# Reordering VectorE in the spectral part, and three small moves at the end of the block loop

## The chip, the cores and the metric

The kernel runs on one core of a Trainium2 chip. The metric is the device time of one launch in microseconds, the median of several runs. Times inside the kernel come from one profiled execution and count from its start. The engines are named as in the profile: PE is TensorE (with PEld for its weight loads), DVE is VectorE, ACT is ScalarE, POOL is GpSimd, SP is SyncE, which only issues transfers here.

## The reference

```python
xn = _layernorm(x)                      # x: 2048 x 512
out = x + fnet(xn) + peer(xn)

def fnet(x):     # real part of a DFT over the hidden and the sequence axis
    a = einsum("bsd,ed->bse", x, dft_hid_re); b = einsum("bsd,ed->bse", x, dft_hid_im)
    return einsum("ts,bse->bte", dft_seq_re, a) - einsum("ts,bse->bte", dft_seq_im, b)

def peer(x):     # 32 heads, two sets of 64 keys, 2 of 64 x 64 = 4096 experts for each head
    q = einsum("nd,dhc->nhc", x, w_q)
    s1 = einsum("nhd,ed->nhe", q[..., :128], k1); s2 = einsum("nhd,ed->nhe", q[..., 128:], k2)
    # best 2 of s1 and of s2, best 2 of their 4 sums: experts top_e, weights g = softmax(top_s)
    act = gelu(einsum("nd,nhkd->nhk", x, u[top_e]))
    return einsum("nhk,nhk,nhkd->nd", g, act, v[top_e])
```

## The kernel before

The kernel has three parts, one after the other, that overlap a little at their borders.

The spectral part takes the first 72 us. The DFT matrices are symmetric, so rows can be added and subtracted in pairs ("folded") ahead of a smaller matmul. The 16 tiles of x are held as four groups g of four tiles, taken in the order G = (1, 0, 2, 3). For each group, `ln` takes statistics (L295, L296), the square root on ScalarE (L300), and a chain of five small VectorE steps up to `rstd` and `negm` (L301 to L305); then ScalarE normalises the four tiles (L317), with two of the first group's on VectorE (L264). `fold(k, g)` adds or subtracts the tiles (L348, into the tile `ft`, which has one buffer), folds twice more (`fold_d`, L332 to L339) and writes the two halves of `Q` (`q`, L351 and L352). `main(k, g)` multiplies Q by the DFT matrix (L371), for k = 0 the cosine part and for k = 1 the sine part. One more row, x5, is folded by `fold_row`. After the last `fold(0, g)` the products are evicted, the scales of the query weights are taken from maxima, and the transposed x (`xpose`) is made for the next part.

The score part computes s = x M for the eight groups of heads (L799), where M is the product of the query weights and the keys, and picks the best two of each set. It ends at 443 us.

The block loop treats 14 blocks of 128 tokens densely, over all 4096 experts; the last two blocks are gathered expert by expert beside it, by GpSimd's transfers. For a block b there are:

- z, in eight steps `cg` of 48 matmuls each (`u_part`, L959), with the GELU on ScalarE (L962);
- four gate products (`g_mm`): VectorE builds two one-hot matrices L (L983) and one weighted R (L991, L994), from the constants io_lam and io_c, and 32 matmuls (L996) put the gates of 32 tokens into PSUM, in one of two buffers;
- four gated products (`w_part`): VectorE multiplies gate and GELU (L1007), ScalarE writes the high half in 16 bits (L1012), VectorE the low half (L1015), which frees the gate's buffer. The two halves are put after the next step, through the list `split`;
- v, in eight steps of 12 matmuls (`v_part`, L1024), which needs all four gated products; and `finish` (L1039), which reads v and adds it to the output row.

The loop runs v of block b and then z of block b + 2. In the steps of v lie the first two gated products of block b + 1 (dictionary `vw`), in those of z its third and fourth (`uw`); `vg` and `ug` place the gate products in the same way. The last two blocks have no z after them.

Beside this the loop checks that the input has the symmetry that the folding assumes and that scaled values stay in range. Those are two streams of small units (`units` with 41, `fit_units` with 60). A call of `paced` in each step of z, and of v of the blocks 1 to 11 and half of block 13, issues so many units that the stream ends with its 94th call: z of the last block with z ends at the 92nd. A unit's load goes to SyncE's queue at once; its work on VectorE (such as L755 and L761) follows two steps later and ScalarE's two after that. `verdict` turns all into a flag, and slower code behind it runs only if the flag is set.

Small tiles in PSUM come from the pools `pc` and `pb`, with two buffers each. In the loop `pc` holds v, two of the eight z steps and one row that the gathered blocks use throughout; `pb` holds the other six z steps and the transposed gates.

The order of the instructions on each engine comes from a planner: it goes through the program as it is traced, and at each point of its own reckoning gives an engine the earliest traced instruction that is ready. An order can be forced with a dependency that makes no semaphore, only an order (`NoSync`). `follow`, `hold` and the new `pace` make such.

## Time and profile before

| what | value |
|---|---|
| median of 3 runs | 1100.72 us (1099.63 to 1101.38) |
| the profiled execution | 1098.52 us, its span 1096.7 us |
| busy share PE, DVE, ACT, POOL | 97%, 87%, 65%, 55% |
| mean granted clock of TensorE | 0.99 |

The span is the time from the first to the last instruction on the core; the time of the execution also has what lies around it. Busy times leave out instructions that only wait, branch or issue transfers. The timeline's rows give start, time, engine, line, operation, what is written and read, and in brackets how long the engine was idle ahead of it and what ended that. A row may merge several like instructions (x22), and its time is then from the first start to the last end. The granted clock is the share of its full speed at which TensorE was let run.

### The profile page before, as it was taken

What the parts mean: (1) busy time and instruction counts of PE and PEld (TensorE: products, weight loads), DVE (VectorE), ACT (ScalarE), POOL (GpSimd) and SP (SyncE); (2) the same over time, 40 slices, a digit from 0 to 9 for tenths busy, and PEclk for the clock granted to TensorE, in tenths of its full rate; (3) what the DMA queues carried; (4) which work ended last, traced back from release to release, by engine and by line L of the source; (5) the groups of instructions that cost most, each with busy time, mean ns of one, the idle gap of its engine ahead of it and who ended that gap; (6) DMA issues with size and microseconds to landing.
All of it is one profiled execution on the core that took longest, in us unless ns stands there. A gap on an engine that the chain in (4) does not pass through costs nothing.

```text
span 1096.7 us, 28484 instructions
## 1 busy us (share of the span) xinstructions
PE 1064.2 (97%) x11070; PEld 694.1 (63%) x11070; DVE 956.3 (87%) x2748; ACT 716.4 (65%) x1326; POOL 600.4 (55%) x553
## 2 busy tenths in 40 slices
PE   5799999999999999999999999999999999999997
PEld 4254555444544544896786867769678585876943
DVE  6879797979999999976998999889999899799971
ACT  3576557688797858542767667677667666767740
POOL 0023446588887955220657476675566657566522
PEclk9799999999999999999999999999999999999998
DMA  8248152445435241272677677766786767676611
GB/s 330 85 152 309 36 196 97 168 141 212 174 125 205 99 160 65 79 257 72 213 227 220 180 217 238 243 213 188 239 252 197 220 204 240 214 226 199 205 35 46
DMA packets 84936, 196.78 MB, mean 179 GB/s; under 512 B 10770, under 2 KB 27559, under 8 KB 84792
## 3 DMA queue, kind: packets, MB, share of 16 engines
q1 hardware_dynamic: 63898, 123.55, 33.5%
q0 software_dynamic: 20736, 71.31, 21.8%
q8 instruction: 88, 1.44, 0.5%
q14 instruction: 56, 0.46, 0.1%
q10 hardware_dynamic: 158, 0.01, 0.0%
HBM read 177.74 MB, written 17.10 MB: 178 GB/s over the span
## 4 chain that ended last, share of the span: by engine, by line
PE 77%; DVE 14%; issue 3%; ACT 2%; DMA 1%; POOL 1%; SPq 0%; DVEq 0%; POOLq 0%; ACTq 0%
PE s L799 25%; PE v L1024 24%; PE z L959 20%; PE g L996 3%; DVE L L983 2%; PE m L147 2%; PE p L371 2%; DVE vals L807 1%; DVE idx L811 1%; DVE act L1015 1%; DMA cx<-in_cb_dram 1%; DVE ga L1066 1%; DVE cx L755 1%; DVE g L1007 1%; DVE R L991 1%
## 5 line engine op out<-in xcount | busy, mean ns | idle before, releaser
L799 PE MATMUL s<-m,xq 128*128 128x512 f16 x1536 | 338.9, 379 | 0.0
L959 PE MATMUL z<-xb,u 128*128 128x128 f16 x5376 | 306.8, 219 | 0.1
L1024 PE MATMUL v<-v,act 128*128 128x512 f16 x1344 | 300.6, 380 | 3.5 <-DVE act L1015 2.6
L959 PEld LDWEIGHTS <-u 128*128 128x128 f16 x5376 | 301.5, 98 | 3.0 <-issue 0.2
L1084 POOL TENSOR_TENSOR ov<-ov,ga 128x512 f32<-128x512 f32 x128 | 180.8, 1413 | 192.0 <-ACT ga L1079 170.4
L799 PEld LDWEIGHTS <-xq 128*128 128x128 f16 x1536 | 148.3, 98 | 171.3 <-issue 0.2
L1024 PEld LDWEIGHTS <-act 128*128 128x128 f16 x1344 | 128.6, 98 | 152.2 <-DVE act L1015 4.1
L983 DVE TENSOR_TENSOR L<-io_lam,cmp 128x2048 f16<-128x2048 f16 x112 | 149.4, 1343 | 37.2 <-PE g L996 37.2
L1050 POOL DMA_INDIRECT ga<-in_uv_dram,eix x128 | 154.9, 1210 | 48.1 <-POOL ov L1084 36.4
L807 DVE MAX8 vals<-ss 128x8 f32<-128x64 f32 x1024 | 152.5, 216 | 16.4 <-ACT ss L804 16.3
L962 ACT ACTIVATE act<-z,scl 128x512 f32<-128x512 f32 x112 | 76.1, 681 | 102.5 <-PE z L959 102.3
L811 DVE FIND_INDEX8 idx<-vals,ss 128x8 uint16<-128x256 f32 x256 | 107.1, 418 | 0.0
L804 ACT ACTIVATE ss<-s,wsc 128x512 f32<-128x512 f32 x112 | 75.5, 680 | 43.3 <-PE s L799 34.0
L1079 ACT ACTIVATE ga<-ga,za 128x512 f32<-128x512 f32 x128 | 92.0, 721 | 9.3 <-ACT za L1077 0.4
L1012 ACT ACTIVATE act<-g 128x1024 f16<-128x1024 f32 x56 | 73.3, 1311 | 24.5 <-DVE g L1007 24.4
L1066 DVE SCALAR_TENSOR_TENSOR ga<-ga,px 128x512 f32<-128x512 f32 x128 | 85.6, 676 | 0.1
L781 ACT ACTIVATE cx<-cx 128x896 f32<-128x896 f32 x64 | 60.6, 946 | 37.7 <-DVE cx L761 19.0
L1015 DVE TENSOR_TENSOR act<-g,act 128x1024 f16<-128x1024 f32 x56 | 72.8, 1301 | 4.6 <-ACT act L1012 4.4
L1007 DVE SCALAR_TENSOR_TENSOR g<-act,scl,g 128x1024 f32<-128x1024 f32 x56 | 71.4, 1279 | 2.3 <-PE g L996 1.4
L169 POOL TENSOR_TENSOR wq<-wq,wh 128x1024 f16<-128x1024 f32 x26 | 55.5, 2135 | 23.7 <-DMA cx<-in_ca_dram 16.1
L991 DVE TENSOR_TENSOR R<-io_c,cmp 128x1024 f16<-128x1024 f16 x56 | 59.6, 1065 | 0.0
L996 PEld LDWEIGHTS <-L 128*128 128x128 f16 x1792 | 51.7, 96 | 8.0 <-DVE act L1015 1.8
(281 smaller groups left out, 1287.8 us busy)
## 6 DMA issues: line engine op xcount, KB each, us to landing
cx<-in_cb_dram SPq DMA_DIRECT2D x50, 448.0 KB
wq<-in_wq_dram SPq DMA_DIRECT2D x32, 512.0 KB
fit<-in_wq_dram SPq DMA_DIRECT2D x28, 512.0 KB
uv<-in_ut_dram SPq DMA_DIRECT2D x16, 512.0 KB
uv<-in_vn_dram SPq DMA_DIRECT2D x16, 512.0 KB
cx<-in_cb_dram SPq DMA_DIRECT2D x28, 224.0 KB
xq<-in_x_dram SPq DMA_DIRECT2D x8, 512.0 KB
xt_d<-xq SPq DMA_DIRECT2D x16, 256.0 KB
```

Of the source, the lines that this page charges most:

```text
L799: mm = nc.tensor.matmul(ps, xt[i][:, l, kd, :], m[:, r, kd, :], start=(n == 0), stop=(n == 3 * KD - 1))
L807: nc.vector.max(vals[:, i, w, :, h], s[:, g, :])
L811: nc.vector.max_index(idx[:, i, w].rearrange("p k h -> p (k h)"), vals[:, i, w, 0:2].rearrange("p k h -> p (k h)"), s[:, w * HC:g + 1, :]. ...
L959: mm = nc.tensor.matmul(p[:, cc * P:(cc + 1) * P], ug[:, l, c % 2, kd, :], xb[:, r, kd, :], start=(n == 0), stop=(n == 3 * KD - 1))
L983: nc.vector.tensor_tensor(L.rearrange("p t (l two) -> p t l two", two=2), io_lam.rearrange("p (l two) -> p l two", two=2).unsqueeze(1).to_ ...
L996: i = nc.tensor.matmul(p[:, hf, t * NC:(t + 1) * NC], L[:, t, :], R[:, hf * 16 + t, :], start=True, stop=True)
L1015: nc.vector.tensor_tensor(w16[..., 1], w, w16[..., 0], op=ALU.subtract)
L1024: mm = nc.tensor.matmul(pv, w16[:, c, :, l], vg[:, r, c % 2, :], start=(c == 0 and k == 0), stop=(c == NC - 1 and k == 2))
L1050: nc.gpsimd.indirect_dma_start(out=t, out_offset=None, in_=uv, in_offset=bass.IndirectOffsetOnAxis(ap=eix[:, n].rearrange("p k h -> p (k h ...
L1066: nc.vector.scalar_tensor_tensor(t, t, 1.0, T["x"], op0=ALU.mult, op1=ALU.mult, accum_out=T["z", n][:, s:s + 1])
L1079: nc.scalar.activation(t, t, AF.Copy, scale=z)
L1084: T["a"] = nc.gpsimd.tensor_tensor(o, o, t, op=ALU.add)
```

## The change

Seven edits in three groups.

In the spectral part: the constants io_lam, io_c, ident16 and not0 are no longer converted on VectorE at the start but after the first group's negm (`constants`), and the iota for two of them comes after the identity on GpSimd. For the groups 0 and 2 the first step of the fold (`fold_t`) is split off; the next group's whole `ln` is traced after it, and the rest of the fold is put behind that group's negm (`end`). The fold of the extra row for k = 1 is put behind the fold traced last (`FF["end"]`).

In the diff, `i` in `fold_d` and in `fold_row` is the first instruction of each.

In the block loop: the fourth gated product of each block with z after it is placed in z's step 3 instead of 4, so that its halves come after step 4 instead of 5. The last block's v is taken from `pb` instead of `pc`.

The checks: the streams end with the 90th call instead of the 94th.

```diff
-    with tc.tile_pool(name="iop", bufs=1, side="right") as iop:
-        iof = iop.tile([P, P], F32, name="iof")
-        nc.gpsimd.iota(iof, pattern=[[1, P]], base=0, channel_multiplier=0,
-                        allow_small_or_imprecise_dtypes=True)
-        nc.vector.tensor_copy(io_lam, iof)
-        nc.vector.tensor_scalar(io_c, iof[:, :NC], float(P), None, op0=ALU.mult)
...
     make_identity(nc, ident)
-    nc.vector.tensor_copy(ident16, ident)
-    nc.vector.tensor_scalar(not0, ident[:, 0:1], -1.0, 1.0, op0=ALU.mult, op1=ALU.add)
+    iof = da.tile([P, P], F32, name="iof")
+    nc.gpsimd.iota(iof, pattern=[[1, P]], base=0, channel_multiplier=0,
+                   allow_small_or_imprecise_dtypes=True)
+
+    def pace(i, after):
+        tc.add_manual_dep(i.ins, after.ins.name, mybir.DependencyInfo(
+            mybir.DependencyClass.NoSync, mybir.DependencyReason.DATA), reason="pace")
+
+    def constants(after):
+        for i in (nc.vector.tensor_scalar(not0, ident[:, 0:1], -1.0, 1.0, op0=ALU.mult, op1=ALU.add),
+                  nc.vector.tensor_copy(ident16, ident), nc.vector.tensor_copy(io_lam, iof),
+                  nc.vector.tensor_scalar(io_c, iof[:, :NC], float(P), None, op0=ALU.mult)):
+            pace(i, after)
...
-        nc.vector.scalar_tensor_tensor(negm[:, g], mvs[:, g, :, 0], -1.0, rstd[:, g], op0=ALU.mult, op1=ALU.mult)
+        end = nc.vector.scalar_tensor_tensor(negm[:, g], mvs[:, g, :, 0], -1.0, rstd[:, g], op0=ALU.mult, op1=ALU.mult)
...
+        return end
...
-    def fold_d(k, t, f, o):
+    def fold_d(k, t, f, o, after=None):
...
+        if after is not None:
+            pace(i, after)
...
+    def fold_t(k, g):
         op = ALU.subtract if k else ALU.add
         t = FF["t"] = da.tile([P, 2, 512], F32, tag="ft", name=f"ft{k}_{g}", bufs=1)
+        nc.vector.tensor_tensor(t, xn[g][:, 0:2], xn[g][:, 2:4], op=op)
+
+    def fold(k, g, after=None):
+        if after is None:
+            fold_t(k, g)
...
-        nc.vector.tensor_tensor(Q[k][g][:, 1, c], o[:, 0, c], o[:, 1, c], op=ALU.subtract)
+        FF["end"] = nc.vector.tensor_tensor(Q[k][g][:, 1, c], o[:, 0, c], o[:, 1, c], op=ALU.subtract)
...
     def fold_row(k):
...
+        if k:
+            pace(i, FF["end"])
...
     for n, g in enumerate(G):
-        ln(g, n)
+        if n == 0:
+            constants(ln(g, n))
+        elif n == 1:
+            ln(g, n)
         if n == 3:
             fold(1, G[0])
             fold_row(0)
             main_row()
-        fold(0, g)
+        if n in (1, 2):
+            fold_t(0, g)
+            fold(0, g, ln(G[n + 1], n + 1))
+        else:
+            fold(0, g)
         main(0, g)
...
-            for f in st[0][st[2]:-(-len(st[0]) * st[1] // (8 * (NB - 2) - 2))]:
+            for f in st[0][st[2]:-(-len(st[0]) * st[1] // (8 * (NB - 2) - 6))]:
...
-            pv = pc(f"v{b}")
+            pv = (pb if b + 1 == NB else pc)(f"v{b}")
             if b + 2 < NB:
-                vw, vg, uw, ug = {0: 0, 4: 1}, {1: 1, 5: 2}, {0: 2, 4: 3}, {1: (1, 3), 5: (2, 0)}
+                vw, vg, uw, ug = {0: 0, 4: 1}, {1: 1, 5: 2}, {0: 2, 3: 3}, {1: (1, 3), 5: (2, 0)}
```

More of the change, by code (lines that the diff above doesn't have):

```diff
@@ L330, in halves @@
             return v.rearrange("p q (s c) -> p q s c", s=2)
-        nc.vector.tensor_tensor(halves(f)[..., 1:P], halves(t[:, :, 0:256])[..., 0:P - 1],
+        i = nc.vector.tensor_tensor(halves(f)[..., 1:P], halves(t[:, :, 0:256])[..., 0:P - 1],
                           halves(t[:, :, 256:512])[..., 1:P], op=op)
+        if after is not None:
+            pace(i, after)
         c = 256 - P * k
@@ L339, in fold_d @@
         nc.vector.tensor_tensor(o[:, :, P + k:2 * P], f[:, :, k:P], f[:, :, P + k:], op=po)
-    def fold(k, g):
+    def fold_t(k, g):
         op = ALU.subtract if k else ALU.add
         t = FF["t"] = da.tile([P, 2, 512], F32, tag="ft", name=f"ft{k}_{g}", bufs=1)
+        nc.vector.tensor_tensor(t, xn[g][:, 0:2], xn[g][:, 2:4], op=op)
+    def fold(k, g, after=None):
+        if after is None:
+            fold_t(k, g)
         f = da.tile([P, 2, 256], F32, tag="ff", name=f"ff{k}_{g}", bufs=2)
         o = FF[k, g] = da.tile([P, 2, 257], F32, tag="fo", name=f"fo{k}_{g}", bufs=2)
-        nc.vector.tensor_tensor(t, xn[g][:, 0:2], xn[g][:, 2:4], op=op)
-        fold_d(k, t, f, o)
+        fold_d(k, FF["t"], f, o, after)
         c = slice(k, 257 - k)
         nc.vector.tensor_tensor(Q[k][g][:, 0, c], o[:, 0, c], o[:, 1, c], op=ALU.add)
-        nc.vector.tensor_tensor(Q[k][g][:, 1, c], o[:, 0, c], o[:, 1, c], op=ALU.subtract)
+        FF["end"] = nc.vector.tensor_tensor(Q[k][g][:, 1, c], o[:, 0, c], o[:, 1, c], op=ALU.subtract)
     def fold_row(k):
         r = da.tile([1, 1, 768], F32, tag="r5", name=f"r5_{k}")
-        nc.vector.tensor_tensor(r[:, 0, 0:512], x5[:, 0], x5[:, 1], op=ALU.subtract if k else ALU.add)
+        i = nc.vector.tensor_tensor(r[:, 0, 0:512], x5[:, 0], x5[:, 1], op=ALU.subtract if k else ALU.add)
+        if k:
+            pace(i, FF["end"])
         fold_d(k, r[:, :, 0:512], r[:, :, 512:], Q[1][0][0:1, 0:1] if k else s5.unsqueeze(1))
```

## The prediction

> **What bounds the kernel now.** I read the page first, then who waited for whom on the TensorE, then the timeline around each of those waits. The page's first line shows a TensorE that is nearly always busy, so a change can only take away its idle time or its slow clock.

> ```profile
> PE 1064.2 (97%) x11070; PEld 694.1 (63%) x11070; DVE 956.3 (87%) x2748; ACT 716.4 (65%) x1326; POOL 600.4 (55%) x553
> ```

> The waits of the TensorE (in all, times, longest) say where the idle time lies:

> ```profile
> PE p L371 <- DVE q L351: 10.0, 4, 3.5
> PE v L1024 <- DVE act L1015: 2.6, 2, 2.1
> PE g L996 <- DVE act L1015: 1.3, 1, 1.3
> PE v L1024 <- DVE y L1039: 0.8, 1, 0.8
> ```

> So there are two places. In the spectral part the matmuls wait four times for VectorE's folds: VectorE is the bound there. In the block loop all that is left is 4.7 us in four waits, each one behind a VectorE result. The change touches all of these. I sum against the profiled execution's 1098.52 us (span 1096.7), which lies 2.2 under the median of 1100.72; the predicted time is that median plus the sum.

> **Spectral part, the constants.** Timeline, columns: start, time from first start to last end, engine, line:

> ```profile
> 8.10 0.68 DVE L295 BATCH_NORM_STATS2 st<-xq 128x6 f32<-128x512 f32 x1
> 9.48 0.43 DVE L80 CAST io_lam<-iof 128x128 f16<-128x128 f32 x1 [0.70 <-POOL iof L78]
> 9.62 0.31 DVE L81 TENSOR_SCALAR io_c<-iof 128x32 f16<-128x32 f32 x1
> 10.31 0.17 DVE L296 BATCH_NORM_AGGREGATE mvs<-st 128x2 f32<-128x6 f32 x1
> 13.40 1.22 DVE L348 TENSOR_TENSOR ft<-xq 128x1024 f32<-128x1024 f32 x1 [0.67 <-ACT xq L317]
> ```

> The last statistics end at 8.10 + 0.68 = 8.78, but their aggregate starts at 10.31, behind four conversions that wait for GpSimd. All later VectorE work of this part hangs on that aggregate. With the conversions moved behind negm it can start at 8.78: **1.53 us sooner**. They cost nothing again: VectorE has 0.67 us free before ft, and without their waits four conversions need about 0.14 us each by the starts at 9.48 and 9.62, some 0.55. If that cover is gone, they cost 0.55. On GpSimd the iota for two of them now comes behind the identity; both were done ahead of the row at 10.31, and are now wanted only after negm, a chain of 1.29 (below) later.

> **Spectral part, the order.** Four groups g (order 1, 0, 2, 3) are normalised and folded; the fourth's fold (0,3) releases the long run of 24 matmuls.

> ```profile
> 14.66 0.69 DVE L332 TENSOR_TENSOR ff<-ft 128x508 f32<-128x508 f32 x1
> 16.59 0.42 DVE L352 TENSOR_TENSOR q<-fo 128x257 f32<-128x257 f32 x1
> 17.05 1.29 DVE L295 BATCH_NORM_STATS2 fo<-xq 128x6 f32<-128x512 f32 x2
> 19.65 0.30 DVE L296 BATCH_NORM_AGGREGATE mvs<-fo 128x2 f32<-128x6 f32 x2
> 19.99 0.30 ACT L300 ACTIVATE sm<-mvs,eps 128x4 f32<-128x4 f32 x1 [5.12 <-DVE mvs L296]
> 21.12 0.16 DVE L305 SCALAR_TENSOR_TENSOR negm<-mvs,rstd 128x4 f32<-128x4 f32 x1
> 24.15 1.51 ACT L320 ACTIVATE x<-x,negm,rstd 1x512 f32<-1x512 f32 x2
> 24.74 1.21 DVE L348 TENSOR_TENSOR ft<-xq 128x1024 f32<-128x1024 f32 x1
> 25.96 0.65 DVE L357 TENSOR_TENSOR r<-x 1x512 f32<-1x512 f32 x1
> 38.84 0.14 DVE L305 SCALAR_TENSOR_TENSOR negm<-mvs,rstd 128x4 f32<-128x4 f32 x1
> 39.02 2.93 ACT L317 ACTIVATE xq<-xq,negm,rstd 128x512 f32<-128x512 f32 x4 [4.51 <-DVE negm L305]
> 41.98 1.23 DVE L348 TENSOR_TENSOR ft<-xq 128x1024 f32<-128x1024 f32 x1 [1.86 <-ACT xq L317]
> 46.32 12.44 PE L371 MATMUL p<-c,q 128*128 128x512 f32 x24 [3.22 <-DVE q L351]
> ```

> From these rows the pieces undisturbed: four statistics 17.05 to 19.95 = 2.90; square root to negm 19.99 to 21.28 = 1.29; ft 1.21; the rest of a fold 14.66 to 17.01 = 2.35. Before, the small steps of one group's negm are spread between another group's folds: the last negm comes at 38.98, VectorE then runs dry for 1.86 while ScalarE normalises (2.93), and only then comes the fourth ft. After, negm of the next group goes ahead of the fold, so ScalarE's 2.93 lies beside fold work.

> Worked out: second ft ends at 24.74 + 1.21 - 1.53 = 24.4. ScalarE is through with the row x at 24.15 + 1.51 - 1.53 = 24.1, so the square root starts there, negm of group 2 ends at 25.4. Fold rest 2.35: 27.8. Statistics of group 3 (2.90), ft of group 2 (1.21), chain 1.29: negm of group 3 at 33.2. The extra row's fold (0.65 and some 0.9 behind it, an estimate from its smaller shapes) goes into the holes of the chains or adds up to 1.6; I take half: 34.0, against 38.98. ScalarE is done at 36.9. From 34.0 VectorE has the rest of (0,2) 2.35, all of fold (1,1) 3.56, since ft has one buffer and is handed on in order, ft 1.21, and 2.0 to the first q: 43.1, against 46.32. That is -3.2; the last two steps of (1,1), 0.7, may fall behind, and the row's fold vanish in holes (-0.8). I take **-3.5 for both edits together**. Ends: -1.0 (order costs 0.5, since a chain with nothing beside it leaves holes: two chains of 1.29) and -5.0 (all filled). After q the run of 24 matmuls, evictions and maxima hang on the same q, so they move along; the score matmuls behind them are dense, so nothing gives it back. The stores of the transposed rows and the loads behind them in SyncE's queue follow the transposes and move with them.

> **Block loop, the fourth gated product.** The one large wait, on its way from z to v:

> ```profile
> 828.04 5.34 PE L1024 MATMUL v<-v,act 128*128 128x512 f16 x24
> 839.60 10.88 PE L959 MATMUL z<-xb,u 128*128 128x128 f16 x192
> 847.00 2.35 DVE L983 TENSOR_TENSOR L<-io_lam,cmp 128x2048 f16<-128x2048 f16 x2
> 850.32 0.95 PE L996 MATMUL g<-R,L 128*128 128x32 f16 x32
> 854.99 1.76 DVE L755 TENSOR_TENSOR cx<-cx 128x256 f32<-128x256 f32 x2 [2.15 <-DMA cx<-in_cb_dram]
> 857.81 1.29 DVE L1015 TENSOR_TENSOR act<-g,act 128x1024 f16<-128x1024 f32 x1
> 859.16 6.56 PE L1024 MATMUL v<-v,act 128*128 128x512 f16 x22 [2.08 <-DVE act L1015]
> 859.00:863.00 4.00, 3.84 (x11) 1.43 (x12) 3.97 (x10) 3.48 (x9) 1.99 (x3) 0.57 0.75 217
> ```

> L1015, the low half of the fourth product, stands in VectorE's queue behind a check (L755) whose transfer is 2.15 late. A step of z is 48 matmuls, 2.7 us by the row of 192; with the halves one step sooner L1015 goes right behind L983, near 849.4, ahead of the check. The 2.08 go. So does what came with them: the last row (a window: PE, PEld, DVE, ACT, POOL busy, then the granted clock) shows 0.57 after the wait, and 22 matmuls took 6.56 where 24 take 5.34, so 22 should take 4.90: 1.66 more. Together **-3.7** (ends 0 and -3.7). What is late next is the check itself; it holds VectorE 0.9 instead of 2.15.

> [...]

> The other such wait, with what VectorE does before it:

> ```profile
> 619.47 2.35 DVE L983 TENSOR_TENSOR L<-io_lam,cmp 128x2048 f16<-128x2048 f16 x2
> 621.54 0.95 PE L996 MATMUL g<-R,L 128*128 128x32 f16 x32
> 628.86 4.92 PE L1024 MATMUL v<-v,act 128*128 128x512 f16 x22 [0.57 <-DVE act L1015]
> 640.00:660.00 20.00, 20.00 (x263) 14.53 (x262) 20.00 (x32) 14.25 (x31) 16.70 (x13) 1.00 0.77 221
> ```

> Here VectorE is full (20.00 of 20). The second L ends at 621.82 and the 17th gate matmul needs it at 621.54 + 0.48 = 622.02: 0.2 to spare. If L1015 (1.29) goes between the two, the gate product waits 1.1; if not, 0.57 are won. I take **0** (ends +1.1 and -0.6).

> **The last blocks.**

> ```profile
> 1049.67 1.02 DVE L755 TENSOR_TENSOR cx<-cx 128x256 f32<-128x256 f32 x2
> 1051.21 1.27 DVE L1015 TENSOR_TENSOR act<-g,act 128x1024 f16<-128x1024 f32 x1
> 1052.53 0.96 PE L996 MATMUL g<-R,L 128*128 128x32 f16 x32 [1.31 <-DVE act L1015]
> 1068.10 20.88 PE L1024 MATMUL v<-v,act 128*128 128x512 f16 x96 [0.84 <-DVE y L1039]
> 1089.02 0.75 DVE L1039 SCALAR_TENSOR_TENSOR y<-v,scl,y 128x512 f32<-128x512 f32 x1 [2.23 <-PE v L1024]
> ```

> Bank: the last v waits 0.84 until VectorE has read the one before out of its bank. The other pair was freed by z long ago: **-0.8** (ends 0, -0.84); the tail behind L1039 moves along. Checks: of 41 units the last was issued in the last z's eighth step and worked on in v of block 12, at 1049.67, ahead of the L1015 for which the gate matmuls wait 1.31. With 90 for 94 steps it is issued eight steps sooner. The wait shrinks by the check's 1.02: **-0.9** (ends 0, -1.31). The price: by 700, some 35 of its steps, 41 units over 90 instead of 94 steps make two thirds of a unit more, 1 to 2 us of VectorE each by the rows of L755, in a stretch that is full: **+0.3** (ends 0, +1.5); its transfers and the halves of u and v read by ScalarE come at most four calls sooner on their queues.

> **Sum:** -3.5 - 3.7 + 0 - 0.8 - 0.9 + 0.3 = **-8.6**: 1089.9 for the profiled execution, 1092.1 for the median. I predict 1092.

> **The rivals.** (1) VectorE stays the bound at the handover: what it is relieved of at L1015 comes back at the next L or check, so that the fourth product gives nothing. For it: 20.00 of 20; against: 847.00's L ends a microsecond before its matmuls. -8.6 + 3.7 = -4.9: 1095.8. (2) The reordering doesn't do what it says: the queue order comes out so that only half of the constants' gain is left (-1.0), and rival 1 holds: -1.0 + 0 - 0.8 - 0.9 + 0.3 = -2.4, at best barely measurable: 1098.3; with the check's wait staying, 1099.2, no change. (3) Slower: L1015 lands between the two L in all twelve z blocks of the loop, and each pays 1.1 as at 621.54: +13.2 - 8.6 = +4.6, 1105.3. It decides from eight blocks on. Against it: at 847.00 both L are done at 849.35, and with 1.29 more the second still ends at 850.64, before the 17th matmul of a gate product that starts at 850.3. (4) More: everything at its good end, -5.0 - 3.7 - 0.6 - 0.8 - 1.3 = -11.4: 1089.3.

> **Chances.** Forecast 0.50 (own range 1090 to 1094.5), rival 4 0.13, rival 1 0.17, rival 2 0.10, rival 3 0.10. A measurement of this kernel can tell about 0.2%, 2.2 us, from no change: faster below 1098.5. Rivals 4 and 1 and the forecast are faster, and rival 2 is split: faster 0.82, same 0.07, slower 0.11. The range takes in rivals 4 and 1, the good end less the 1.1 by which the fastest run lies under the median, and the better half of rival 2: 1088 to 1098.5.

> **What would show it.** The first mvs aggregate near 8.8 and the four conversions after negm; the fourth ft near 39, without a wait for ScalarE; 24 matmuls starting near 43; L1015 before the next L1012 by a step, no wait of v for it, and a clock of 1.00 through 850 to 870; no wait of v for y; the wait of g at 1051 under 0.5. The prediction is wrong if g waits for L in many blocks, if the fourth ft still waits for ScalarE, or if the run of 24 starts after 45.

## The result, and the profile after

In six runs each, the kernel before took 1100.27 us in the median (1098.56 to 1103.19) and the changed one 1092.67 us (1091.40 to 1094.45). The ratio is 0.9936, with a 95% interval of 0.9913 to 0.9958: 7.0 us less, give or take 2.5. The forecast was 1092.0. The profiled execution of the changed kernel took 1093.28 us (span 1091.4), 5.2 less than that of before. So part of the gain between the medians does not show between the two traces; the profiled execution of before was one of its better ones.

The first line of the page after, and who waited for whom on TensorE (us in all, times, longest):

```profile
PE 1062.2 (97%) x11070; PEld 694.0 (64%) x11070; DVE 979.0 (90%) x2748; ACT 716.2 (66%) x1326; POOL 603.7 (55%) x553
```

```profile
PE p L385 <- DVE q L363: 7.7, 3, 4.9
PE z L980 <- DVE y L1060: 2.0, 3, 1.1
PE g L1017 <- DVE L L1004: 1.6, 3, 0.7
PE g L1017 <- DVE act L1036: 0.9, 1, 0.9
PE m L141 <- POOL wq L163: 0.9, 1, 0.9
```

The lines have new numbers: L1060 is the `y` of `finish` (L1039 before), L1004 the L (L983), L1036 the low half (L1015), L353 the first step of a fold (L348), L776 a check's work (L755). Both waits of v, for the low half and for y, are gone. New are a wait of z for y, which I had not thought of, and a longer one of the gate product for L. Where the time went, by the first matmul of each part:

| from the start to | before | after | difference |
|---|---|---|---|
| first score matmul | 72.45 | 69.43 | -3.03 |
| first z matmul, the start of the block loop | 443.89 | 441.45 | -2.44 |
| end of the last v matmul | 1088.98 | 1084.87 | -4.11 |
| end of the span | 1096.72 | 1091.38 | -5.34 |

The spectral part gains 3.0 and gives 0.6 back in the score part; the block loop gains 1.7; after the last matmul 1.2 more go. The timeline after (start, time, engine, line), first the spectral part with the one wait of the score part:

```profile
8.82 0.18 DVE L301 BATCH_NORM_AGGREGATE mvs<-st 128x2 f32<-128x6 f32 x1
12.03 1.23 DVE L353 TENSOR_TENSOR ft<-xq 128x1024 f32<-128x1024 f32 x1 [0.19 <-ACT xq L322]
24.72 0.67 DVE L369 TENSOR_TENSOR r<-x 1x512 f32<-1x512 f32 x1
26.77 0.16 DVE L310 SCALAR_TENSOR_TENSOR negm<-mvs,rstd 128x4 f32<-128x4 f32 x1
33.91 0.16 DVE L310 SCALAR_TENSOR_TENSOR negm<-mvs,rstd 128x4 f32<-128x4 f32 x1
38.58 1.22 DVE L353 TENSOR_TENSOR ft<-xq 128x1024 f32<-128x1024 f32 x1
43.46 12.11 PE L385 MATMUL p<-c,q 128*128 128x512 f32 x24 [0.85 <-DVE q L363]
86.50 0.20 PE L141 MATMUL m<-sums,wq 128*128 128x64 f16 x1 [0.88 <-POOL wq L163]
```

It went as worked out: the aggregate at 8.82 (before 10.31), the extra row's fold in the hole of a chain, the last negm at 33.91, the fourth ft at 38.58 with no wait for ScalarE, the run of 24 at 43.46. Then the loop, with four of its waits:

```profile
620.08 0.56 PE L1017 MATMUL g<-R,L 128*128 128x32 f16 x16 [0.73 <-DVE L L1004]
621.21 0.56 PE L1017 MATMUL g<-R,L 128*128 128x32 f16 x16 [0.57 <-DVE L L1004]
702.47 1.72 PE L980 MATMUL z<-xb,u 128*128 128x128 f16 x28 [1.15 <-DVE y L1060]
853.65 1.30 DVE L1036 TENSOR_TENSOR act<-g,act 128x1024 f16<-128x1024 f32 x1
854.85 1.90 DVE L776 TENSOR_TENSOR cx<-cx 128x256 f32<-128x256 f32 x2
1049.42 0.97 PE L1017 MATMUL g<-R,L 128*128 128x32 f16 x32 [0.92 <-DVE act L1036]
```

At 853.65 the low half goes ahead of the check that had held it up, and the check's load is no longer late. Two windows over the whole loop, of before and of after, in this order (us, then busy time and count of PE, PEld, DVE, ACT, POOL, the granted clock, the share of DMA, GB/s):

```profile
443.90:1089.00 645.10, 640.02 (x8551) 478.62 (x8548) 568.66 (x876) 409.10 (x851) 351.72 (x276) 1.00 0.64 196
```

```profile
441.50:1084.90 643.40, 638.62 (x8551) 478.75 (x8547) 588.78 (x876) 409.28 (x851) 355.29 (x276) 1.00 0.65 196
```

TensorE is idle for 645.10 - 640.02 = 5.1 before and 643.40 - 638.62 = 4.8 after. So in these two traces the waits were exchanged, not saved. What fell is TensorE's busy time, by 1.4, and the slow clock after the wait at 857 (0.50 from 859.09 to 862.50), 1.7 by the forecast's reckoning, accounts for that. The forecast's three gains in the loop cannot all have come as they were argued, although the total fits.

### The profile page after: what moved, and what is told of

Its sections match the earlier page's. It is cut to its first block, busy times and chain, and to the rows that moved or that the text cites. A ratio compares the mean times of both kernels' runs of the same rounds, so it can differ in the third digit from the quotient of the medians.

```text
span 1091.4 us, 28485 instructions
## 1 busy us (share of the span) xinstructions
PE 1062.2 (97%) x11070; PEld 694.0 (64%) x11070; DVE 979.0 (90%) x2748; ACT 716.2 (66%) x1326; POOL 603.7 (55%) x553
## 5 line engine op out<-in xcount | busy, mean ns | idle before, releaser
L1105 POOL TENSOR_TENSOR ov<-ov,ga 128x512 f32<-128x512 f32 x128 | 177.7, 1388 | 185.3 <-ACT ga L1100 164.5
L1071 POOL DMA_INDIRECT ga<-in_uv_dram,eix x128 | 162.1, 1266 | 48.4 <-POOL ov L1105 35.5
L1004 DVE TENSOR_TENSOR L<-io_lam,cmp 128x2048 f16<-128x2048 f16 x112 | 159.5, 1438 | 17.7 <-PE g L1017 17.7
L983 ACT ACTIVATE act<-z,scl 128x512 f32<-128x512 f32 x112 | 75.6, 680 | 92.0 <-PE z L980 88.5
L1036 DVE TENSOR_TENSOR act<-g,act 128x1024 f16<-128x1024 f32 x56 | 72.9, 1301 | 7.9 <-ACT act L1033 7.4
L1015 DVE TENSOR_TENSOR R<-R,cmp 128x1024 f16<-128x1024 f16 x56 | 59.4, 1062 | 1.4
```

Source lines behind the costliest of these rows:

```text
L1004: nc.vector.tensor_tensor(L.rearrange("p t (l two) -> p t l two", two=2), io_lam.rearrange("p (l two) -> p l two", two=2).unsqueeze(1).to_ ...
L1036: nc.vector.tensor_tensor(w16[..., 1], w, w16[..., 0], op=ALU.subtract)
L1071: nc.gpsimd.indirect_dma_start(out=t, out_offset=None, in_=uv, in_offset=bass.IndirectOffsetOnAxis(ap=eix[:, n].rearrange("p k h -> p (k h ...
L1105: T["a"] = nc.gpsimd.tensor_tensor(o, o, t, op=ALU.add)
```

## Experiments

All ratios are to the kernel before, run on the same chip beside it; 0.001 is 1.1 us.

**The spectral part alone, then its constants alone.** The first kernel is the changed one with the loop's three edits taken back; the second also has the old order:

```diff
-            for f in st[0][st[2]:-(-len(st[0]) * st[1] // (8 * (NB - 2) - 6))]:
+            for f in st[0][st[2]:-(-len(st[0]) * st[1] // (8 * (NB - 2) - 2))]:
...
-            pv = (pb if b + 1 == NB else pc)(f"v{b}")
+            pv = pc(f"v{b}")
...
-                vw, vg, uw, ug = {0: 0, 4: 1}, {1: 1, 5: 2}, {0: 2, 3: 3}, {1: (1, 3), 5: (2, 0)}
+                vw, vg, uw, ug = {0: 0, 4: 1}, {1: 1, 5: 2}, {0: 2, 4: 3}, {1: (1, 3), 5: (2, 0)}
```

```diff
-        if k:
-            pace(i, FF["end"])
...
-        elif n == 1:
+        else:
             ln(g, n)
...
-        if n in (1, 2):
-            fold_t(0, g)
-            fold(0, g, ln(G[n + 1], n + 1))
-        else:
-            fold(0, g)
+        fold(0, g)
```

> The changed kernel with the three edits of the block loop undone: only the constants and the order of the spectral part are left. Theory A (the parts add): the run of 24 matmuls starts near 43.5, where it does with all edits, the first scores 3.0 us earlier than before, 0.6 of it given back at the first weight product, so 2.4 us faster than before, near 1097.9 beside 1100.3; the block loop keeps the waits of before, v for the low half 2.6 us in all, v for y 0.8. Theory B (the spectral part's gain is lost behind it, the whole gain is the loop's): within 1 us of before, although the run of 24 starts earlier.

> Of all edits only the constants behind negm; the order of folds and chains as before. My prediction's step: the first aggregate at 8.8, everything behind it 1.5 us sooner, the run of 24 matmuls near 44.8, the time 1.0 to 1.5 us lower than before. Rival: the chains wait for ScalarE and for normalised tiles anyway, and the run of 24 starts at 45.8 or later: under 0.5 us.

Measured: 0.9963 (0.9935 to 0.9990) for both edits, 0.9982 (0.9957 to 1.0007) for the constants alone. The timeline of the first, then of the second:

```profile
43.55 12.26 PE L385 MATMUL p<-c,q 128*128 128x512 f32 x24 [0.85 <-DVE q L363]
```

```profile
37.68 0.14 DVE L310 SCALAR_TENSOR_TENSOR negm<-mvs,rstd 128x4 f32<-128x4 f32 x1
40.82 1.23 DVE L353 TENSOR_TENSOR ft<-xq 128x1024 f32<-128x1024 f32 x1 [1.86 <-ACT xq L322]
45.16 13.48 PE L383 MATMUL p<-c,q 128*128 128x512 f32 x24 [1.53 <-DVE q L363]
```

The run of 24 comes at 43.55 and at 45.16, against 46.32. So in these traces the constants give 1.2 of what I put at 1.53, and the order another 1.6; in the other kernels with the old spectral part the run starts at 46.5 to 47.2, in those with the new one at 43.5 to 44.1. With the constants alone the fourth ft waits its old 1.86 for ScalarE; only the order takes that away. How long the 24 then run hangs on the clock: they take 12.26 with half clock for 3.4 us of it, 13.48 with 5.9, and 12.44 with 3.8 in before; less half of these times, that is 10.5 to 10.6 in each (an estimate). The 0.6 that I expected to be given back in the score part did not show in the kernel with the spectral part alone. Over all kernels of this study, the start of the block loop lies 0.5 us after that of before in the mean of the six with the old spectral part, before itself among them (-0.3 to +1.3), and 2.9 ahead of it in the mean of the seven with the new one (1.6 to 4.5). That makes 3.4, and the interval of the ratio 1.1 to 7.2; the forecast had 3.5.

**The loop alone.** The kernel before with the three loop edits:

```diff
-            for f in st[0][st[2]:-(-len(st[0]) * st[1] // (8 * (NB - 2) - 2))]:
+            for f in st[0][st[2]:-(-len(st[0]) * st[1] // (8 * (NB - 2) - 6))]:
...
-            pv = pc(f"v{b}")
+            pv = (pb if b + 1 == NB else pc)(f"v{b}")
...
-                vw, vg, uw, ug = {0: 0, 4: 1}, {1: 1, 5: 2}, {0: 2, 4: 3}, {1: (1, 3), 5: (2, 0)}
+                vw, vg, uw, ug = {0: 0, 4: 1}, {1: 1, 5: 2}, {0: 2, 3: 3}, {1: (1, 3), 5: (2, 0)}
```

> The kernel before with the three edits of the block loop and nothing of the spectral part. Theory A: the wait of v for the low half and the slow clock behind it go (3.7 us), the bank and the checks give 1.4, new waits of g for L and of z for y take 3 back: 2 to 3 us faster than before in a profiled run that had the clock's fall, 4 to 5 in the median if runs of before fall more often. Theory B: the waits are only exchanged, and all that is left is the end of the loop: 1.0 to 1.4 us faster.

Measured: 0.9947 (0.9920 to 0.9973), or 5.8 us; the forecast's terms for the loop sum to 5.1. With the spectral part's 0.0037 that would be 0.0090 in all, where 0.0064 was measured; the intervals, some 0.0027 for each half, leave room for that.

**The fourth gated product alone.** This is the edit to which I gave 3.7, on the kernel before:

```diff
-                vw, vg, uw, ug = {0: 0, 4: 1}, {1: 1, 5: 2}, {0: 2, 4: 3}, {1: (1, 3), 5: (2, 0)}
+                vw, vg, uw, ug = {0: 0, 4: 1}, {1: 1, 5: 2}, {0: 2, 3: 3}, {1: (1, 3), 5: (2, 0)}
```

> The kernel before with only the fourth gated product a step sooner. My prediction's step: no wait of v for the low half, no fall of the clock behind one, 3.7 us less in the profiled execution, with one new wait of g for L near 620 of at most 1.1; z does not wait for y. Rival: the low half only changes places with other work of a full VectorE, z waits for y or g for L by as much as v had waited, and the time stays within 1.5 us of before.

Measured: 1.0006 (0.9987 to 1.0025). By itself it gives nothing that can be told, and the 3.7 lie outside the interval. The wait at 857 and its slow clock do go (3.9 us less from v of block 8 to v of block 9), but others come. TensorE's waits in that kernel, then its timeline at the costliest:

```profile
PE g L996 <- DVE act L1015: 2.9, 1, 2.9
PE z L959 <- DVE y L1039: 2.6, 1, 2.6
PE g L996 <- DVE L L983: 1.4, 2, 1.1
```

```profile
652.72 1.30 DVE L1015 TENSOR_TENSOR act<-g,act 128x1024 f16<-128x1024 f32 x1
655.71 1.99 DVE L983 TENSOR_TENSOR L<-io_lam,cmp 128x2048 f16<-128x2048 f16 x1
657.76 0.56 PE L996 MATMUL g<-R,L 128*128 128x32 f16 x16 [1.10 <-DVE L L983]
658.56 1.43 DVE L1157 TENSOR_TENSOR cx<-cx 128x128 f32<-128x128 f32 x1
660.11 0.74 DVE L1039 SCALAR_TENSOR_TENSOR y<-v,scl,y 128x512 f32<-128x512 f32 x1
660.90 7.32 PE L959 MATMUL z<-xb,u 128*128 128x128 f16 x99 [2.58 <-DVE y L1039]
```

With the low half at 652.72, all that VectorE does behind it comes later: the second L (1.10 of wait), and y, which reads v out of the bank pair that z's third step is to write. z waits 2.58 for it, and TensorE runs at half clock for 3.41 after that. At 1055 the gate product waits 2.93 for the low half where it had waited 1.31. The wait of z for y can't be put down to this edit alone, though: the two kernels with the spectral part alone and with the bank alone, whose checks and fourth product stand as before, each have one of 1.6.

**The faster checks: taken back from the changed kernel, and alone on the kernel before.**

```diff
-            for f in st[0][st[2]:-(-len(st[0]) * st[1] // (8 * (NB - 2) - 6))]:
+            for f in st[0][st[2]:-(-len(st[0]) * st[1] // (8 * (NB - 2) - 2))]:
```

```diff
-            for f in st[0][st[2]:-(-len(st[0]) * st[1] // (8 * (NB - 2) - 2))]:
+            for f in st[0][st[2]:-(-len(st[0]) * st[1] // (8 * (NB - 2) - 6))]:
```

> The changed kernel with the checks spread over 94 calls again. My prediction's step: the last check stands again ahead of the low half for which g waits near 1048, so that wait grows by 0.9 at least from its 0.92; the full stretch is relieved by 0.3 us. Sum +0.6. If the new waits of z for y come from the faster checks, they are gone here, and the time is 1 to 2 us lower than the changed kernel's.

> The kernel before with one edit: the checks' steps spread over 90 calls in place of 94. Theory (the faster checks carry the block loop's gain, since their loads come in time at the head of VectorE's queue): VectorE's waits for check loads fall from 7.1 us to under 3, the wait of v for the low half at 857 (2.08) and the slow clock behind it go (-3.7 from block 8 to 9), and the wait of g at 1051 shrinks; some 1 to 2 us come back as waits of z for y elsewhere. In all -2 to -5 us, ratio 0.9955 to 0.998. Rival (the fourth product carries it, as I forecast): the wait at 857 stays within 0.5 us and the ratio is 0.999 to 1.0005.

Measured: the changed kernel without them 0.9969 (0.9951 to 0.9987), against 0.9936 with them; alone 0.9989 (0.9973 to 1.0005). So they give 3.6 where the fourth product has been moved (give or take 3, by the two intervals), and 1.2, which cannot be told from nothing, where it has not (2 to 5 were expected there). I had put them at 0.6. What they do is seen in VectorE's waits for the loads of checks (line waited for, us, times, longest), of before, of the changed kernel without the faster checks, and of the changed kernel itself:

```profile
DVE cx L755 <- DMA cx<-in_cb_dram: 7.1, 3, 2.9
```

```profile
DVE cx L776 <- DMA cx<-in_cb_dram: 9.8, 4, 3.4
```

```profile
DVE sums L1177 <- DMA cx<-in_wt_dram: 2.5, 1, 2.5
```

Both kinds of load together make VectorE wait for 7.1 to 11.9 in all six kernels with 94 calls and checks two steps behind their loads, and for 1.0 to 3.8 in the seven with 90 calls. I take it that the units fall at other steps, away from other transfers; which transfers held the loads up I have not shown. With the faster checks alone, the wait at 857 vanishes too, although the low half stands where it stood, two places behind a check. That check's load is now in time:

```profile
862.50 1.01 DVE L755 TENSOR_TENSOR cx<-cx 128x256 f32<-128x256 f32 x2
864.58 1.31 DVE L1015 TENSOR_TENSOR act<-g,act 128x1024 f16<-128x1024 f32 x1
865.29 5.58 PE L1024 MATMUL v<-v,act 128*128 128x512 f16 x24
```

But z now waits for y:

```profile
703.40 2.08 DVE L994 TENSOR_TENSOR R<-R,cmp 128x1024 f16<-128x1024 f16 x1
705.40 0.94 DVE L755 TENSOR_TENSOR cx<-cx 128x768 f32<-128x768 f32 x1
707.08 0.74 DVE L1039 SCALAR_TENSOR_TENSOR y<-v,scl,y 128x512 f32<-128x512 f32 x1
707.88 3.41 PE L959 MATMUL z<-xb,u 128*128 128x128 f16 x33 [2.45 <-DVE y L1039]
```

That is 4.2 lost from v of block 4 to v of block 5, slow clock included, against 3.7 won at 857.

**The fourth product taken back from the changed kernel.**

```diff
-                vw, vg, uw, ug = {0: 0, 4: 1}, {1: 1, 5: 2}, {0: 2, 3: 3}, {1: (1, 3), 5: (2, 0)}
+                vw, vg, uw, ug = {0: 0, 4: 1}, {1: 1, 5: 2}, {0: 2, 4: 3}, {1: (1, 3), 5: (2, 0)}
```

> The changed kernel with the fourth gated product put back a step later. If the earlier product is what carries the loop's gain: v waits again for the low half in one to three blocks, 1 to 3 us slower than the changed kernel. If the new waits (z for y, 2.0 us in three blocks, g for L, 1.3) come from the earlier product, they are gone here, and the time is the changed kernel's within 1 us; if they come from the faster checks, they stay, and the time is 3 us or more above it.

Measured: 0.9942 (0.9916 to 0.9967), against 0.9936: nothing that can be told in this direction either, though the two intervals alone would leave room for the 3.7. The trace speaks against that: there is no wait over 0.5 for the low half anywhere, and at 1050 the gate product does not wait at all.

**The bank alone.**

```diff
-            pv = pc(f"v{b}")
+            pv = (pb if b + 1 == NB else pc)(f"v{b}")
```

> The kernel before with only the last block's v in the other pool. My prediction's step: the wait of 0.84 between the last two v goes, everything behind moves with it, 0.8 us less; nothing else in the trace changes. Rival: the end hangs on the checks' flag or the gathered blocks instead, and the time stays. In the time itself 0.8 is less than five rounds tell; the trace decides by the last v's start after the end of the one before, and by what lies between its end and the end of the span (7.7 before).

Measured: 0.9986 (0.9962 to 1.0009), too little to tell; in the trace the 0.84 is gone and v of block 12 to v of block 13 is 1.0 shorter, as forecast. But the rest of the trace did change, against what was expected: TensorE idles for 8.7 in the loop where it idled for 5.1, although the code up to the last v is that of before.

**z takes v's banks a step later.** If z waits for y because its third step writes what y reads, the fourth and seventh step should not wait. On the changed kernel, then the same with the fourth product put back:

```diff
-            p = (pc if cg in ((2, 3, 6, 7) if b == 0 else (2, 5)) else pb)(f"z{b}_{cg}")
+            p = (pc if cg in ((2, 3, 6, 7) if b == 0 else (3, 6)) else pb)(f"z{b}_{cg}")
```

```diff
-            p = (pc if cg in ((2, 3, 6, 7) if b == 0 else (2, 5)) else pb)(f"z{b}_{cg}")
+            p = (pc if cg in ((2, 3, 6, 7) if b == 0 else (3, 6)) else pb)(f"z{b}_{cg}")
...
-                vw, vg, uw, ug = {0: 0, 4: 1}, {1: 1, 5: 2}, {0: 2, 3: 3}, {1: (1, 3), 5: (2, 0)}
+                vw, vg, uw, ug = {0: 0, 4: 1}, {1: 1, 5: 2}, {0: 2, 4: 3}, {1: (1, 3), 5: (2, 0)}
```

> The changed kernel, with the z steps 3 and 6 instead of 2 and 5 in the pool from which v also takes its bank. z's first step in that pool then comes 2.7 us later after v, and VectorE has this much more time to read v out. If the waits of z for y (2.0 us and some 0.2 beside) are what this bank costs: none is left and the time is 1.5 to 2.2 us under the changed kernel's. Rival: the same VectorE work is late for the next gate product instead; g waits for L by as much, and the time stays.

> The changed kernel with the bank pair of v taken at the fourth and seventh step of z, and the fourth gated product put back to where it was before. Theory (that product's place is worth nothing by itself once the checks are faster): within 1.5 us of the same kernel with the product a step sooner (median 1091.94), ratio 0.991 to 0.9945. Rival (its place carries the 3.7 us that I forecast): the wait of v for the low half near 857 is back with over 1.5 us and a slow clock, ratio 0.995 to 0.997.

Measured: 0.9920 (0.9891 to 0.9948) and 0.9932 (0.9911 to 0.9953). Neither can be told from the changed kernel. The waits of z for y are gone from both, which shows their cause; in their place v waits for the last step's GELU, which in ScalarE's queue stands behind the sums of a check and the work of a gathered block. Shortly before, ScalarE itself had waited at the head of its queue for the load of a check of ranges, 4.69 us in the first kernel and 2.28 in the second. TensorE's waits of the first and of the second:

```profile
PE v L1045 <- ACT act L983: 2.9, 2, 2.6
```

```profile
PE v L1045 <- ACT act L983: 2.3, 2, 1.3
```

**Checks three steps behind their loads.** If late loads at the head of VectorE's queue are what holds the low half up, more time for a load should do as well as the faster checks. The edit moves the work of the checks in L755 (L776) and leaves the others where they are. On the kernel before, and on the changed kernel together with z's later step:

```diff
-                after(2, work)
+                after(3, work)
```

```diff
-                after(2, work)
+                after(3, work)
...
-            p = (pc if cg in ((2, 3, 6, 7) if b == 0 else (2, 5)) else pb)(f"z{b}_{cg}")
+            p = (pc if cg in ((2, 3, 6, 7) if b == 0 else (3, 6)) else pb)(f"z{b}_{cg}")
```

> The kernel before with one edit: VectorE's work of a check comes three steps behind the issue of its load in place of two, so that each load has a step, some 2.7 us, more. The pace stays at 94 calls and the fourth product stays where it was. Theory (what held the low half back was a late load at the head of VectorE's queue): VectorE's waits for check loads fall from 7.1 us to under 2, the wait of v at 857 and its slow clock go (-3.7), ratio 0.995 to 0.998. Rival (the place of the halves in the queue decides, or the loads only start later because their buffers come free later): the waits for loads stay above 5 us, v waits over 1.5 us somewhere, ratio 0.999 to 1.001.

> The changed kernel with two edits: in a block's z the two steps that take the bank pair of v are the fourth and seventh in place of the third and sixth (z then waits for y a step later), and a check's VectorE work comes three steps behind its load in place of two. Theory: the first edit takes away z's waits for y (1.15 at 701, 0.70 at 931), the second the late load of 3.1 us that came up at 946 when the first edit stood alone and cost 2.8 us there; together 1 to 4 us less than the changed kernel, ratio to before 0.989 to 0.993. Rival: the loads lie longer in their buffers, start later and are late as before, or the halves now fall at other places: no better than the changed kernel, ratio 0.993 to 0.996.

Measured: 0.9981 (0.9969 to 0.9994), 2.1 us less, on the kernel before. VectorE's wait for check loads falls from 7.1 to 0.7, and the wait at 857 with its clock goes (3.7 less there). But the check changes its place too, and now stands behind the low half:

```profile
855.82 1.30 DVE L1015 TENSOR_TENSOR act<-g,act 128x1024 f16<-128x1024 f32 x1
858.15 2.10 DVE L755 TENSOR_TENSOR cx<-cx 128x256 f32<-128x256 f32 x2
```

This run alone does not tell the late load from the check's place. The kernel with the faster checks alone does: the check is still ahead of the low half, only its load is in time, and v does not wait. So the late load was needed for that wait, and any of three edits removes it: an earlier low half, faster checks, later checks. The four kernels with none of them (before, the two spectral ones, the bank alone) take 48.1 to 50.4 us from v of block 8 to v of block 9, the ten others 45.5 to 46.5. But 5.6 come back elsewhere in the loop of that trace, 2.9 of them at 1053. The timeline there:

```profile
1051.79 1.27 DVE L1015 TENSOR_TENSOR act<-g,act 128x1024 f16<-128x1024 f32 x1
1053.12 0.97 PE L996 MATMUL g<-R,L 128*128 128x32 f16 x32 [2.51 <-DVE act L1015]
```

The other kernel, meant as the best one, came out at 0.9966 (0.9948 to 0.9984), worse than the changed kernel. No z waits for y, and VectorE waits 3.0 for check loads (3.8 with z's later step alone), but the gate product now waits for L five times, 6.9 in all, and after two of these waits TensorE runs at half clock. At the one of them at 819.82 (2.54 us, then 0.50 from 820.3 to 823.7) the L that it waits for took 2.89, where an L takes 1.21 at other places.

**All together.** The loop from the first z matmul to the end of the last v, in the 14 profiled executions: its length, TensorE's idle time in it, and how many stretches of 3.41 us at half clock it has.

| kernel | length | idle | slow | ratio |
|---|---|---|---|---|
| before | 645.1 | 5.1 | 1 | 1 |
| spectral part alone | 645.9 | 7.3 | 0 | 0.9963 |
| constants alone | 646.3 | 6.3 | 1 | 0.9982 |
| fourth product alone | 647.5 | 7.8 | 1 | 1.0006 |
| bank alone | 648.5 | 8.7 | 1 | 0.9986 |
| faster checks alone | 648.3 | 7.4 | 1 | 0.9989 |
| checks three steps behind | 647.0 | 6.5 | 1 | 0.9981 |
| loop alone (three edits) | 642.7 | 4.4 | 0 | 0.9947 |
| changed | 643.4 | 4.8 | 0 | 0.9936 |
| changed, old pace of checks | 648.0 | 6.8 | 2 | 0.9969 |
| changed, fourth product back | 645.2 | 6.1 | 0 | 0.9942 |
| changed, z's later step | 645.2 | 5.3 | 1 | 0.9920 |
| the same, fourth product back | 643.9 | 5.3 | 0 | 0.9932 |
| the same as the last but one, checks three steps behind | 649.6 | 7.9 | 2 | 0.9966 |

Length less idle less 1.7 for each slow stretch (half of its 3.41, an estimate) is 637.8 to 639.2 in every row. That I take to be the work; by this reckoning an edit changes only the waits and the number of slow stretches behind them. The first three rows run the same loop code, and the bank alone differs from them only in the last v; these four lie up to 3.4 apart, so one trace does not rank two kernels that lie closer than that.

## Why the prediction was right or wrong

The time, the range and the direction were right (1092.67 for 1092.0), and so was the spectral part; of the loop the sum was right and its parts were not. That was luck: the fourth product alone gave nothing where I had 3.7, the checks gave 3.6 beside it where I had 0.6, and the two errors cancel.

**Spectral part, -3.5: right.** The ends of the working came within half a microsecond: 33.9 for 34.0, and 43.5 for 43.1. Between them two errors cancel: the fourth ft came at 38.6, where the sum of the pieces gives 39.9 (34.0 + 2.35 + 3.56) and the signs said 39, and from its end to the run of 24 it took 3.7 instead of 2.0, for the last two steps of fold (1,1) and the ft of the next fold went in between. The means over 13 traces give 3.4. The constants' share was 1.2 instead of 1.53. That the score matmuls "give nothing back" was not quite right: the first product of query weights and keys waited 0.29 for GpSimd before and 0.88 after; in three of the seven kernels with the new spectral part there is no such wait.

**Fourth gated product, -3.7: wrong.** Alone it measured +0.06% (-0.13 to +0.25), and taking it back cost 0.06%: nothing that can be told. The step that failed is "with the halves one step sooner ... the 2.08 go", taken as a saving. They do go, and the slow clock with them. (The low half did not land right behind L either: it came 3.2 us ahead of v's start, at 853.65, where 849.4 would have been 7.1 ahead; still ahead of the check.) But I named as late next only the check, and priced no other instruction that an earlier low half pushes back on a VectorE with no room: the second L, the low half at 1052, and y, for which z waits through the bank. Rival 1, that what VectorE is relieved of comes back at the next L, was right about this edit, and wrong about the sum. The 2.08 themselves had another cause, the late load, which other edits remove as well.

**The other handover, 0: right within its ends.** The wait of 0.57 for the low half went and 0.73 + 0.57 for L came: the step with "0.2 to spare" was the right place to look.

**Bank, -0.8: right,** by the trace: the wait is gone.

**Checks, -0.9 + 0.3: mis-sized.** With the fourth product moved they gave 3.6 (give or take 3), not 0.6. I looked at the one check ahead of the low half at 1051, and at their load on VectorE, and not at the loads: that 7.1 us of VectorE's time went in waiting for them stood in the profile, and with 90 calls it is 2.5. At 1051 the term was right alone, the 1.31 go wholly; the fourth product puts 0.92 back. So the mark "under 0.5" was missed.

**The clock term, 1.66 for a wait of 2.08: right for this wait.** It does not hold for every wait of that length: after one of 2.43 in the kernel with the spectral part alone the clock stayed at 1.00 (last section).

**What remains open.** The 1.2 after the last matmul: the tail is 7.6 to 7.7 us long in before, the two spectral kernels and that with faster checks alone, and 6.5 to 6.8 in all others. The bank is not the cause, for the tail is short with the fourth product alone and with later checks alone too. In every trace the span ends 1.1 to 1.3 us after the last transfer of the two queues that the page calls `instruction`; that transfer ends 6.2 to 6.6 us after the last matmul in the four, and 5.3 to 5.7 in the others. Why it comes later in the four is not shown. And how the loop's edits act together: the four edits alone sum to -0.37 + 0.06 - 0.14 - 0.11 = -0.56%, and -0.64% was measured. The traces show each loop edit alone trading waits and the three together having the fewest, but by the times an interplay is no more than possible.

**What the sum was made against.** It was -8.6 from one profiled execution, and between the two profiled ones it is -5.2; I added it to the median, and between the medians it is -7.6. The two other kernels with the same loop code idle for 7.3 and 6.3 in it, and that with the bank alone for 8.7, where the profiled execution of before idles for 5.1: what it loses in a usual run is probably more than its trace shows.

## What to carry to other kernels

Where one engine with an ordered queue is full, a wait that ends at one of its results is not a saving until each result behind the moved instruction has been followed to its reader; add up the idle time of the bounding engine over the whole stage before and after, and only what is missing there is won. Look for the instruction that is itself waiting at the head of that queue (here one for a late load). By the times, taking that wait away did at most a little more (2.1 us with later checks, 1.2 with faster ones, which cannot be told from nothing) than moving the delayed instruction (nothing that can be told): it too moved work, and much came back as other waits. And a short wait cost more than its length where the clock fell after it (2.08 us and some 1.66 more in before). In the loops measured here the clock fell after steps of 3.413 us with 2.01 us or more of idle time and after none with 1.70 or less (next section), so two waits of 1 us in different steps should be a gain over one of 2 within a step; that is an estimate from these numbers, and no run tried it by itself.

## What the runs showed of the hardware

```profile
856.60:860.00 3.40, 0.76 (x5) 0.15 (x3) 3.40 (x5) 1.08 (x3) 2.84 (x4) 1.00 0.90 187
860.00:863.40 3.40, 3.40 (x10) 1.20 (x9) 3.37 (x6) 3.29 (x9) 1.85 (x1) 0.50 0.61 184
```

```profile
853.60:857.00 3.40, 2.48 (x39) 1.98 (x36) 2.81 (x3) 2.65 (x6) 2.74 (x3) 1.00 1.02 262
857.00:860.40 3.40, 1.89 (x9) 0.90 (x10) 3.40 (x7) 1.74 (x5) 3.13 (x2) 1.00 0.97 231
860.40:863.80 3.40, 3.40 (x37) 1.80 (x34) 3.37 (x6) 2.01 (x6) 1.47 (x2) 1.00 0.74 215
```

In the first TensorE is busy for 0.76 of 3.40 and runs at 0.50 next; in the second for 2.48 and 1.89, and the clock stays at 1.00. So a wait of much the same length cost some 1.7 us more in one run than in the other (an estimate, half of 3.41).

**Some L and R take longer beside GpSimd's sums.** The 224 instructions that write L and R take 258.5 us before and 272.0 after, though they are the same. Some of them take over 0.2 us more than the 1.21 (L) or 0.68 (R) that is usual here: 49 before, together 45 us more, and 62 after, together 59 more. Every one of these overlaps a `tensor_tensor` of GpSimd (the sum of a gathered block, L1084 before and L1105 after). But 44 others before and 30 after overlap one too, by up to 1.21 us, and are not longer by 0.2. Two of after's R, and GpSimd's sum that runs beside the second:

```profile
545.91 0.68 DVE L1012 TENSOR_TENSOR R<-io_c,cmp 128x1024 f16<-128x1024 f16 x1
546.63 2.04 DVE L1015 TENSOR_TENSOR R<-R,cmp 128x1024 f16<-128x1024 f16 x1
546.84 1.27 POOL L1105 TENSOR_TENSOR ov<-ov,ga 128x512 f32<-128x512 f32 x1
```

0.68 becomes 2.04, longer by the 1.27 of GpSimd's sum and a little more. L1036, of which one input lies in PSUM, takes 1.27 to 1.34 in all its 56 places, though 27 of them overlap such a sum. What makes the difference is not shown. That the moves of the change shifted L and R beside GpSimd's sums is how I read the 62 against 49. I had counted 1.2 for each L; they took up to 2.84.
